# Storing one chunk last, with its MoE rows added by one-hot matmuls, in a channel-attention and mixture-of-depths kernel

## Chip, cores and metric

The kernel runs on one core of a Trainium2 chip. The metric is the device time of one execution in microseconds (us), the median of several runs. The core has TensorE (PE; its weight loads are listed apart as PEld), VectorE (DVE), ScalarE (ACT), GpSimd (POOL) and SyncE (SP), which work side by side and wait for each other by semaphores, and 16 DMA engines, which all transfers share.

## What is computed

Four batches of q, k and v, each 6208 rows by 256 channels, go through attention among the channels. The result goes through a mixture-of-depths layer: in each batch, the 128 rows with the highest score get an MLP added.

```python
# B, N, C = 4, 6208, 256;  F = 1024;  capacity = 128
qn = q / (norm(q, axis=1) + 1e-6);  kn = k / (norm(k, axis=1) + 1e-6)
a = softmax(kn.transpose(0, 2, 1) @ qn / tau)     # 256 x 256 for each batch
x = v @ a
scores = x @ w_gate
out = x.copy()
for b in range(B):
    top = indices of the 128 highest scores[b]
    xe = x[b, top]
    ye = maximum(xe @ w1, 0) @ w2
    out[b, top] = xe + sigmoid(scores[b, top])[:, None] * ye
```

## The kernel before

A batch has six chunks of 1024 rows (8 rows in each of 128 partitions) and a rest of 64 rows. Pass 1 reads q and k and accumulates k'q and the norms. A softmax of 256 x 256 follows. Pass 2 reads v, transposes it, multiplies it by the attention matrix `a_sb`, and stages the rows for the store. Beside that a selection (a search for the threshold in 7 steps on VectorE, with a small matmul in each) finds the 128 rows of the batch. They are gathered from v, go through the MLP, and are scattered over the rows that are already stored. So a scatter must come after the stores of its own batch.

All loads are issued by GpSimd and cast from float32 to bfloat16 on the way. All stores are issued by SyncE. GpSimd issues strictly in the order of the program.

```python
QK_BUFS = 4;  V_BUFS = 6;  ST_BUFS = 7;  EARLY = 4;  HOLD = 3
...
T = [("T", L, g, a) for g, a in zip(gs, [1, 1, 1, 0, 1, 1, 0, 1, 0, 1, 0, 1, 0])]  # transposes, last batch
S = [("S", L, g) for g in gs]                                                       # its scores
plan += [("tail",)] + T[:2] + [("warm", L, 6)] + T[2:3] + [("warm", L, 6)] + T[3:4]
plan += [("adv",), ("a", L)]
for i in range(4, 7):
    plan += [T[i], ("warm", L, 8)]
plan += [T[7], ("warm", L, 4), T[8], T[9]] + S[:4] + [("warm", L, 4)] + T[10:] + [("side",)] + S[4:]
...
def emit_weights():                       # issued by GpSimd behind the first loads of q and k
    nc.gpsimd.dma_start(out=w1_sb, in_=moe_w1.rearrange("(dc p) f -> p dc f", p=P))
    nc.gpsimd.dma_start(out=w2_sb, in_=moe_w2.rearrange("(fc p) d -> p fc d", p=P))
...
def keep_warm(n):                         # matmuls whose result nobody reads
    bank = ps_o.tile([P, 2, C], F32, name="o_ps")
    for _ in range(n):
        nc.tensor.matmul(bank[:, 0, 0:P], lhsT=ident_b, rhs=ones_b, start=True, stop=True)
...
def between():                            # after each pair of output rows: a step of the selection or MLP
    if now[0] > B:
        pairs[0] += 1
        if pairs[0] % 5 in (0, 3) and not advance(side):
            advance_all(side2)
...
# pass 2: outputs of two rows of each partition at a time
for pj in range(m):
    for cc in range(2):
        nc.tensor.matmul(o_ps[:parts, pj, :], lhsT=vt_sb[:, cc, j, :parts], rhs=a_sb[:, cc, :], ...)
if now[0] > B and not side and pairs[0] % 2 == 1:
    nc.vector.tensor_copy(st[...], o_ps[:parts, :m, :])
else:
    nc.scalar.copy(st[...], o_ps[:parts, :m, :])
between()
...
# the end of the MLP of batch b
upd = moe.tile([P, D], F32, name="upd", bufs=2)
nc.vector.scalar_tensor_tensor(out=upd, in0=y_ps[:, 0, :], scalar=gate, in1=xe, op0=ALU.mult, op1=ALU.add)
yield
yield
while held[b] or (b >= E - 1 and deferred):
    yield
nc.gpsimd.indirect_dma_start(out=out_flat[0:(b + 1) * N, :],
                             out_offset=bass.IndirectOffsetOnAxis(ap=idx[:, 0:1], axis=0), in_=upd, ...)
...
# the tail, after the last loads of v
b = B - 1
side.append(select_stages(b))
advance(side)
flush_deferred()                          # the stores held back: three of batch 1, two of batch 2
...
now[0] = B + 1
pairs[0] = 1
for op in rest:                           # outputs of batch 2 (E) from the third chunk on
    do_out(E, op[2], False)
for g in gs:                              # outputs of batch 3
    do_out(b, g, False)
while side:
    advance(side)
...
keep_warm(32)
while side2:                              # MLP and scatter of batch 3
    advance(side2)
```

Of the kernel before, what the change touches and what calls it, by code (L numbers as in the profile page):

```python
# [9 lines left out]
F32 = mybir.dt.float32  # L10
BF16 = mybir.dt.bfloat16
# [6 lines left out]
P = 128  # L18
# [8 lines left out]
def kernel(  # L27
# [72 lines left out]

    gs = [g for ci in range(NFULL + 1) for g in groups(ci)]
    E = B - 2

    def mixed(b, ci, extra):

# [7 lines left out]
    def pass2(b):  # L113
        ops = [("T", b, gs[0], 1), ("T", b, gs[1], 1), ("a", b)]
        for i, g in enumerate(gs):
            ops.append(("O", b, g, True))
# [24 lines left out]

    T = [("T", L, g, a) for g, a in zip(gs, [1, 1, 1, 0, 1, 1, 0, 1, 0, 1, 0, 1, 0])]
    S = [("S", L, g) for g in gs]
    plan += [("tail",)] + T[:2] + [("warm", L, 6)] + T[2:3] + [("warm", L, 6)] + T[3:4]
    plan += [("adv",), ("a", L)]
    for i in range(4, 7):
        plan += [T[i], ("warm", L, 8)]
    plan += [T[7], ("warm", L, 4), T[8], T[9]] + S[:4] + [("warm", L, 4)] + T[10:] + [("side",)] + S[4:]
    units = []
    for op in plan:  # L150
        if op[0] in ("p1", "T"):
# [51 lines left out]

    pump(4)


    ident_f = const.tile([P, P], F32)
    make_identity(nc, ident_f)
# [46 lines left out]
    ones_col = const.tile([P, NCOL], BF16)  # L255
    nc.vector.memset(ones_col, 1.0)

    w1_sb = const.tile([P, C // P, F], BF16)
    w2_sb = const.tile([P, NFC, D], BF16)

    def emit_weights():
        nc.gpsimd.dma_start(out=w1_sb, in_=moe_w1.rearrange("(dc p) f -> p dc f", p=P))
        nc.gpsimd.dma_start(out=w2_sb, in_=moe_w2.rearrange("(fc p) d -> p fc d", p=P))

    pump()
    emit_weights()


    acc = {}
# [28 lines left out]
    def softmax_stages(b):  # L298
        s_ps, g_ps = acc[b]
        s_sb = smx.tile([P, 2, C], F32, name="s_sb")  # L300
        nc.scalar.copy(s_sb, s_ps)  # L301
        junk = smx.tile([P, P], F32, name="junk")
        nsq = smx.tile([P, 4], F32, name="nsq")
        for i in range(4):
            nc.vector.tensor_tensor_reduce(out=junk, in0=g_ps[:, i, :], in1=ident_f, scale=1.0,  # L305
                                           scalar=0.0, op0=ALU.mult, op1=ALU.add,
                                           accum_out=nsq[:, i:i + 1])


# [29 lines left out]
        e = smx.tile([P, 2, C], F32, name="e")  # L339
        rsum = smx.tile([P, 2], F32, name="rsum")  # L340
        aw = smx.tile([P, 2], F32, name="aw")
        for cc in range(2):
            ss = smx.tile([P, C], F32, name=f"ss{cc}")
            nc.vector.tensor_tensor(out=ss, in0=s_sb[:, cc, :], in1=rq_ps[:, 0:C], op=ALU.mult)
            nc.scalar.activation(e[:, cc, :], ss, AF.Exp, scale=rn[:, 2 + cc:3 + cc],
                                 accum_out=rsum[:, cc:cc + 1])
# [19 lines left out]
    stage_of = {}  # L366
    deferred = []
    gate_done = []
    held = {b: NFULL + 1 for b in range(B)}
    side = []  # L370
    side2 = []
    waiting = []
# [19 lines left out]
    def p2_transpose(b, g, on_act=False):  # L392
        ci, s0, n = g
        parts = P if ci < NFULL else REM
        vt = loaded[("v", b, ci)][0]
        vt_ps = vt_psum()
        for j in range(n):
            for cc in range(2):
                nc.tensor.transpose(vt_ps[:, cc, j, :parts], in_=vt[:parts, s0 + j, cc * P:(cc + 1) * P],  # L399
                                    identity=ident_b[:parts, :parts])  # L400
        vt_sb = vt_pool.tile([P, 2, 4, P], BF16, name="vt_sb")
# [51 lines left out]
    def p2_out(b, g, vt_sb, scores):  # L453
# [9 lines left out]
        for pair in range((n + 1) // 2):  # L463
# [13 lines left out]
                nc.scalar.copy(st[:parts, s0 + pair * 2:s0 + pair * 2 + m, :], o_ps[:parts, :m, :])  # L477
            between()

    def emit_store(b, ci):  # L480
        st = stage_of.pop((b, ci))
        if ci < NFULL:
            return nc.sync.dma_start(out=view(out, b, ci), in_=st)
        return nc.sync.dma_start(out=view(out, b, ci), in_=st[:REM, 0, :])


    gathered = {}

    def select_stages(b):

# [97 lines left out]
    def mlp_stages(b):  # L588
# [44 lines left out]
        for fc in range(NFC):  # L633
            nc.tensor.matmul(y_ps[:, 0, :], lhsT=h_sb[:, fc, :], rhs=w2_sb[:, fc, :], start=fc == 0,
                             stop=fc == NFC - 1)
        upd = moe.tile([P, D], F32, name="upd", bufs=2)
        nc.vector.scalar_tensor_tensor(out=upd, in0=y_ps[:, 0, :], scalar=gate, in1=xe, op0=ALU.mult,
                                       op1=ALU.add)
        yield
        yield  # L640
        while held[b] or (b >= E - 1 and deferred):
            yield
        nc.gpsimd.indirect_dma_start(out=out_flat[0:(b + 1) * N, :],
                                     out_offset=bass.IndirectOffsetOnAxis(ap=idx[:, 0:1], axis=0),
                                     in_=upd, in_offset=None)


    smx_side = []
# [85 lines left out]
    for op in plan:  # L734
# [16 lines left out]
        elif kind == "a":  # L751
            while b not in a_tiles:
                advance(smx_side)
        elif kind == "side":
            while side:
                advance(side)
# [66 lines left out]
```

## Time and profile before

| what | value |
|---|---|
| time, median of 3 runs (lowest to highest) | 269.53 us (269.02 to 269.69) |
| span of the profiled run | 266.5 us |
| TensorE busy | 203.4 us (76% of the span) |
| VectorE busy | 119.9 us (45%) |
| ScalarE busy | 76.7 us (29%) |
| GpSimd busy | 57.2 us (21%) |
| moved by the DMA engines | 65.92 MB, mean 247 GB/s |
| read from HBM, written to HBM | 79.04 MB, 25.95 MB |

The page divides the span into 40 slices of 6.66 us; each digit is the busy share of a slice in tenths. GB/s counts the bytes that the transfers deliver, so a load that casts float32 to bfloat16 counts half of what it reads. In the chain of waits, each line is a start, a duration and what was waited for; it runs back from the last instruction to what released it. A "stretch" is a part of the span between two times, with the busy time of each engine, the granted share of TensorE's clock, the DMA share and GB/s. "POOLq" and "SPq" are the sequencers of those engines, which wait and issue and are not counted as busy.

### The profile page before, as it was taken

What the parts mean: (1) busy time and instruction counts of PE and PEld (TensorE: products, weight loads), DVE (VectorE), ACT (ScalarE), POOL (GpSimd) and SP (SyncE); (2) the same over time, 40 slices, a digit from 0 to 9 for tenths busy, and PEclk for the clock granted to TensorE, in tenths of its full rate; (3) what the DMA queues carried; (4) which work ended last, traced back from release to release, by engine and by line L of the source; (5) the groups of instructions that cost most, each with busy time, mean ns of one, the idle gap of its engine ahead of it and who ended that gap; (6) DMA issues with size and microseconds to landing.
All of it is one profiled execution on the core that took longest, in us unless ns stands there. A gap on an engine that the chain in (4) does not pass through costs nothing.

```text
span 266.5 us, 6120 instructions
## 1 busy us (share of the span) xinstructions
PE 203.4 (76%) x2604; PEld 179.1 (67%) x2604; DVE 119.9 (45%) x466; ACT 76.7 (29%) x140; POOL 57.2 (21%) x106
## 2 busy tenths in 40 slices
PE   0587278899965866799997896899998798899710
PEld 0476267789954656689986785889987586678500
DVE  0200001714415356614438845774866745867500
ACT  1000000157730000137651001533004545885300
POOL 7322213121110023222201343220431011010110
PEclk9999959999989799799997999999999985899995
DMA  6999999999999999999999999999999999999920
GB/s 112 214 211 209 213 212 211 215 213 264 314 317 313 312 218 214 215 213 224 318 314 228 212 218 218 212 215 213 213 209 214 202 361 404 421 408 406 419 76 0
DMA packets 17642, 65.92 MB, mean 247 GB/s; under 512 B 2000, under 2 KB 4688, under 8 KB 14544
## 3 DMA queue, kind: packets, MB, share of 16 engines
q0 software_dynamic: 13696, 39.98, 76.0%
q1 hardware_dynamic: 3920, 25.56, 23.6%
q8 instruction: 20, 0.33, 0.4%
q14 instruction: 6, 0.05, 0.0%
HBM read 79.04 MB, written 25.95 MB: 394 GB/s over the span
## 4 chain that ended last, share of the span: by engine, by line
DMA 54%; PE 23%; issue 9%; DVE 7%; POOL 2%; ACT 1%; POOLq 1%; SPq 0%
DMA k_ch<-in_k_dram 29%; DMA q_ch<-in_q_dram 17%; DMA v_ch<-in_v_dram 6%; PE s_ps L286 5%; PE o_ps L469 5%; DMA out_dram<-stage_rem 3%; PE g_ps L290 2%; PE g_ps L288 2%; PE vt_ps L399 2%; PE s_ps L469 2%; PE sc_ps L424 1%; DVE cnt L532 1%; PE g_ps L469 1%; DVE cmp L528 1%; DVE junk L305 1%
## 5 line engine op out<-in xcount | busy, mean ns | idle before, releaser
L286 PE MATMUL s_ps<-q_ch,k_ch 128*128 128x256 bf16 x384 | 96.0, 290 | 30.1 <-DMA k_ch<-in_k_dram 28.9
L288 PE MATMUL g_ps<-q_ch 128*128 128x128 bf16 x384 | 88.3, 230 | 1.6 <-DVE nsq L305 1.6
L290 PE MATMUL g_ps<-k_ch 128*128 128x128 bf16 x384 | 88.2, 230 | 0.0
L286 PEld LDWEIGHTS <-k_ch 128*128 128x128 bf16 x384 | 39.9, 104 | 34.7 <-DMA k_ch<-in_k_dram 31.8
L469 PE MATMUL o_ps<-a_sb,vt_sb 128*128 128x256 bf16 (+1 forms) x310 | 47.6, 279 | 1.5 <-ACT vt_sb L403 1.3
L477 ACT COPY stage<-o_ps 128x512 f32<-128x512 f32 x76 | 42.8, 588 | 19.7 <-PE o_ps L469 17.2
L290 PEld LDWEIGHTS <-k_ch 128*128 128x128 bf16 x384 | 39.9, 104 | 8.8 <-issue 2.1
L288 PEld LDWEIGHTS <-q_ch 128*128 128x128 bf16 x384 | 39.9, 104 | 1.7 <-issue 1.4
L469 PEld LDWEIGHTS <-vt_sb 128*128 128x128 bf16 x392 | 32.2, 101 | 9.0 <-issue 3.5
L405 DVE COPY vt_sb<-vt_ps 128x1024 bf16<-128x1024 bf16 (+1 forms) x35 | 22.2, 637 | 31.9 <-PE vt_ps L399 31.8
L301 ACT COPY s_sb<-s_ps 128x512 f32<-128x512 f32 x4 | 2.3, 586 | 105.9 <-PE s_ps L286 105.9
L424 PEld LDWEIGHTS <-vt_sb 128*128 128x128 bf16 x392 | 25.4, 97 | 2.7 <-DVE u L495 0.2
L399 PEld LDWEIGHTS <-v_ch 128*128 128x128 bf16 x384 | 22.3, 97 | 5.9 <-DMA v_ch<-in_v_dram 4.7
L399 PE MATMUL vt_ps<-ident_b,v_ch 128*128 128x128 bf16 x336 | 24.7, 219 | 1.6 <-DMA v_ch<-in_v_dram 0.9
L424 PE MATMUL sc_ps<-aw_sb,vt_sb 128*128 128x2 bf16 x392 | 25.8, 164 | 0.0
L305 DVE CUSTOM_DVE_ANT_0 junk<-g_ps,ident_f 128x128 f32<-128x128 f32 x16 | 4.7, 291 | 41.8 <-PE g_ps L290 41.4
L174 POOL DMA_DIRECT2D q_ch<-in_q_dram x23 | 12.8, 555 | 49.1 <-PE g_ps L290 18.5
L174 POOL DMA_DIRECT2D k_ch<-in_k_dram x23 | 12.6, 546 | 27.9 <-DMA k_ch<-in_k_dram 8.8
L174 POOL DMA_DIRECT2D v_ch<-in_v_dram x24 | 12.8, 539 | 24.2 <-DMA k_ch<-in_k_dram 11.5
L532 DVE TENSOR_REDUCE cnt<-cmp 128x7 bf16<-128x343 bf16 x28 | 14.4, 513 | 1.0
L528 DVE SCALAR_TENSOR_TENSOR cmp<-u,delta,shares 128x343 bf16<-128x343 f32 x24 | 13.9, 579 | 0.9
L403 ACT COPY vt_sb<-vt_ps 128x1024 bf16<-128x1024 bf16 x11 | 10.6, 1012 | 12.3 <-PE vt_ps L399 12.2
(138 smaller groups left out, 199.8 us busy)
## 6 DMA issues: line engine op xcount, KB each, us to landing
out_dram<-stage SPq DMA_DIRECT2D x24, 1024.0 KB, 9.1
v_ch<-in_v_dram POOLq DMA_DIRECT2D x24, 512.0 KB, 14.9
q_ch<-in_q_dram POOLq DMA_DIRECT2D x23, 512.0 KB, 17.2
k_ch<-in_k_dram POOLq DMA_DIRECT2D x23, 512.0 KB, 18.5
w_sb<-in_moe_w_dram POOLq DMA_DIRECT2D x2, 512.0 KB, 19.9
q_ch<-in_q_dram POOLq DMA_DIRECT2D x2, 256.0 KB, 9.7
k_ch<-in_k_dram POOLq DMA_DIRECT2D x2, 256.0 KB, 10.4
out_dram<-stage_rem SPq DMA_DIRECT2D x4, 64.0 KB, 6.7
```

The source lines that it names most:

```text
L174: ins = nc.gpsimd.dma_start(out=t, in_=view(src, b, ci))
L286: nc.tensor.matmul(s_ps[:, cc, :], lhsT=ks[:, sl], rhs=qs, start=first and cc == 0, stop=last and cc == 1)
L288: nc.tensor.matmul(g_ps[:, cc, :], lhsT=qs[:, sl], rhs=qs[:, sl], start=first and cc == 0, stop=False)
L290: nc.tensor.matmul(g_ps[:, 2 + cc, :], lhsT=ks[:, sl], rhs=ks[:, sl], start=False, stop=last and cc == 1)
L399: nc.tensor.transpose(vt_ps[:, cc, j, :parts], in_=vt[:parts, s0 + j, cc * P:(cc + 1) * P], identity=ident_b[:parts, :parts])
L403: nc.scalar.copy(vt_sb[:, :, :n, :parts], vt_ps[:, :, :n, :parts])
L405: nc.vector.tensor_copy(vt_sb[:, :, :n, :parts], vt_ps[:, :, :n, :parts])
L424: nc.tensor.matmul(sc_ps[:parts, col, :], lhsT=vt_sb[:, cc, j, :parts], rhs=aw_sb[:, cc, :], start=cc == 0 and col in (0, NCOL - 1), stop= ...
L469: nc.tensor.matmul(o_ps[:parts, pj, :], lhsT=vt_sb[:, cc, j, :parts], rhs=a_sb[:, cc, :], start=pj == 0 and cc == 0, stop=pj == m - 1 and ...
L477: nc.scalar.copy(st[:parts, s0 + pair * 2:s0 + pair * 2 + m, :], o_ps[:parts, :m, :])
L528: nc.vector.scalar_tensor_tensor(out=cmp, in0=wide, scalar=delta, in1=thr, op0=ALU.subtract, op1=ALU.is_ge)
L532: nc.vector.tensor_reduce(out=cnt, in_=cmp, axis=AX.X, op=ALU.add)
```

## The change

Four things are changed together.

1. One chunk of batch 1, the last full one, is not computed in pass 2 of its batch. Its transposed v is kept in a buffer of its own (`vt_late`). Its outputs are computed in the tail, and its store is issued last of all, behind the stores of batch 3. The scatter of batch 1 runs before that store, so the store must bring the MoE rows with it: for each of the 8 rows of a partition, a one-hot matrix of 128 x 128 says which selected row belongs there, and three matmuls of it with the MLP's result, split into three bfloat16 parts, are added to the outputs in PSUM. The purpose is that the transfers have something to do while the last scatter waits for the stores of batch 3.
2. The MoE weights are loaded in float32 by SyncE ahead of everything into two staging buffers, and ScalarE casts them.
3. A store and a scatter of different batches are declared independent.
4. The dummy matmuls of the tail are fewer (the one-hot pairs stand in their place), the selection of the last batch takes its steps sooner, and the softmax works in place, which frees space.

```diff
-    plan += [("tail",)] + T[:2] + [("warm", L, 6)] + T[2:3] + [("warm", L, 6)] + T[3:4]
-    plan += [("adv",), ("a", L)]
-    for i in range(4, 7):
-        plan += [T[i], ("warm", L, 8)]
-    plan += [T[7], ("warm", L, 4), T[8], T[9]] + S[:4] + [("warm", L, 4)] + T[10:] + [("side",)] + S[4:]
+    plan += [("tail",)] + T[:2] + [("late", H, 0)] + T[2:4] + [("adv",), ("a", L)]
+    plan += T[4:8] + [("late", H, 1)] + T[8:10] + S[:4] + [("warm", L, 4)] + T[10:] + [("side",)] + S[4:]
...
+    def emit_weights():
+        for dst, src, inner in ((w1_sb, moe_w1, F), (w2_sb, moe_w2, D)):
+            raw = st_pool.tile([P, RPP, C], F32, name="stage").rearrange("p a c -> p (a c)")
+            raw = raw.rearrange("p (k n) -> p k n", n=inner)
+            nc.sync.dma_start(out=raw, in_=src.rearrange("(k p) n -> p k n", p=P))
+            nc.scalar.copy(dst, raw)
+    emit_weights()
...
-            if pairs[0] % 5 in (0, 3) and not advance(side):
+            due = pairs[0] in (2, 4, 6) or pairs[0] > 6 and pairs[0] % 5 in (0, 3)
+            if due and not advance(side):
...
+    def late_pair(k):
+        ...
+        for pj in range(2):
+            for cc in range(2):
+                nc.tensor.matmul(o_ps[:, pj, :], lhsT=vts[(H, g)][:, cc, k % 2 * 2 + pj, :], rhs=a_sb[:, cc, :],
+                                 start=pj == 0 and cc == 0, stop=False)
+            for i in range(3):
+                nc.tensor.matmul(o_ps[:, pj, :], lhsT=onehot[:, row + pj, :], rhs=parts[:, i, :],
+                                 start=False, stop=pj == 1 and i == 2)
+        nc.scalar.copy(st[:, row:row + 2, :], o_ps)
+    def late_rows(b, idx, gy):
+        base = float(b * N + (NFULL - 1) * CHUNK)
+        at = moe.tile([P, 1], F32, name="late_at")
+        nc.gpsimd.tensor_copy(at, idx)
+        nc.gpsimd.tensor_scalar(out=at, in0=at, scalar1=-base, scalar2=1.0 / RPP, op0=ALU.add, op1=ALU.mult)
+        at_row = moe.tile([P, RPP], F32, name="late_at_row")
+        nc.gpsimd.tensor_scalar(out=at_row, in0=iota_row[:, 0:RPP], scalar1=-1.0 / RPP, scalar2=at, ...)
+        onehot = moe.tile([P, RPP, P], BF16, name="late_onehot")
+        for s in range(RPP):
+            nc.gpsimd.tensor_scalar(out=onehot[:, s, :], in0=iota_row, scalar1=at_row[:, s:s + 1], ..., op0=ALU.is_equal)
+        parts = moe.tile([P, 3, D], BF16, name="late_parts")
+        for i in range(3):
+            nc.gpsimd.tensor_copy(parts[:, i, :], gy)
+            if i < 2:
+                nc.gpsimd.tensor_tensor(out=gy, in0=gy, in1=parts[:, i, :], op=ALU.subtract)
...
+        for o, sca in scatters:
+            if o != b:
+                tc.declare_no_dep(ins.ins, sca.ins, reason="rows of different batches")
...
-        nc.vector.scalar_tensor_tensor(out=upd, in0=y_ps[:, 0, :], scalar=gate, in1=xe, op0=ALU.mult, op1=ALU.add)
+        if b == H:                            # H = batch 1
+            gy = moe.tile([P, D], F32, name="gy")
+            nc.vector.tensor_scalar(out=gy, in0=y_ps[:, 0, :], scalar1=gate, scalar2=None, op0=ALU.mult)
+            nc.gpsimd.tensor_tensor(out=upd, in0=gy, in1=xe, op=ALU.add)
+            late_rows(b, idx, gy)
+        else:
+            nc.vector.scalar_tensor_tensor(...)
...
     side.append(select_stages(b))
     advance(side)
+    advance(side)
     flush_deferred()
...
-    pairs[0] = 1
     for op in rest:
         do_out(E, op[2], False)
-    for g in gs:
+    for i, g in enumerate(gs):
         do_out(b, g, False)
+        if i in (8, 9):
+            late_pair(i - 6)
+    emit_store(H, NFULL - 1)
...
-    keep_warm(32)
+    keep_warm(8)
```

More of the change, by code (lines that the diff above doesn't have):

```diff
@@ L102 @@
     E = B - 2
+    H = B - 3
+    late = [(NFULL - 1, 0, 4), (NFULL - 1, 4, 4)]
     def mixed(b, ci, extra):
@@ L115, in pass2 @@
         for i, g in enumerate(gs):
-            ops.append(("O", b, g, True))
+            ops.append(("S", b, g) if b == H and g in late else ("O", b, g, True))
             if i + 2 < len(gs):
@@ L204 @@
     pump(4)
+    w1_sb = const.tile([P, C // P, F], BF16)
+    w2_sb = const.tile([P, NFC, D], BF16)
+    def emit_weights():
+        for dst, src, inner in ((w1_sb, moe_w1, F), (w2_sb, moe_w2, D)):
+            assert C * F == P * RPP * C
+            raw = st_pool.tile([P, RPP, C], F32, name="stage").rearrange("p a c -> p (a c)")
[3 more added lines that the diff above has]
+    emit_weights()
     ident_f = const.tile([P, P], F32)
@@ L256 @@
     nc.vector.memset(ones_col, 1.0)
[L258 to L263, printed above, removed]
     pump()
-    emit_weights()
     acc = {}
@@ L338, in softmax_stages @@
                          start=True, stop=True)
-        e = smx.tile([P, 2, C], F32, name="e")
+        e = s_sb
         rsum = smx.tile([P, 2], F32, name="rsum")
@@ L342, in softmax_stages @@
         for cc in range(2):
[L343 to L345 removed]
+            nc.vector.tensor_tensor(out=e[:, cc, :], in0=e[:, cc, :], in1=rq_ps[:, 0:C], op=ALU.mult)
+            nc.scalar.activation(e[:, cc, :], e[:, cc, :], AF.Exp, scale=rn[:, 2 + cc:3 + cc],
                                  accum_out=rsum[:, cc:cc + 1])
@@ L368 @@
     gate_done = []
-    held = {b: NFULL + 1 for b in range(B)}
+    held = {b: NFULL + 1 - (b == H) for b in range(B)}
     side = []
@@ L400, in p2_transpose @@
                                     identity=ident_b[:parts, :parts])
-        vt_sb = vt_pool.tile([P, 2, 4, P], BF16, name="vt_sb")
+        if b == H and g in late:
+            vt_sb = moe.tile([P, 2, 4, P], BF16, name="vt_late", bufs=2)
+        else:
+            vt_sb = vt_pool.tile([P, 2, 4, P], BF16, name="vt_sb")
         if on_act:
@@ L478, in p2_out @@
             between()
+    def late_pair(k):
+        g = late[k // 2]
+        onehot, parts = late_moe
+        if k == 0:
+            stage_of[(H, NFULL - 1)] = st_pool.tile([P, RPP, C], F32, name="stage")
+        st = stage_of[(H, NFULL - 1)]
+        a_sb = a_tiles[H][0]
+        o_ps = out_psum()
+        row = g[1] + k % 2 * 2
+        for pj in range(2):
[6 more added lines that the diff above has]
+        nc.scalar.copy(st[:, row:row + 2, :], o_ps)
@@ new lines @@
+    late_moe = []
+    def late_rows(b, idx, gy):
[4 more added lines that the diff above has]
+        at_row = moe.tile([P, RPP], F32, name="late_at_row")
+        nc.gpsimd.tensor_scalar(out=at_row, in0=iota_row[:, 0:RPP], scalar1=-1.0 / RPP, scalar2=at,
+                                op0=ALU.mult, op1=ALU.add)
+        onehot = moe.tile([P, RPP, P], BF16, name="late_onehot")
+        for s in range(RPP):
+            nc.gpsimd.tensor_scalar(out=onehot[:, s, :], in0=iota_row, scalar1=at_row[:, s:s + 1],
+                                    scalar2=None, op0=ALU.is_equal)
+        parts = moe.tile([P, 3, D], BF16, name="late_parts")
[3 more added lines that the diff above has]
+                nc.gpsimd.tensor_tensor(out=gy, in0=gy, in1=parts[:, i, :], op=ALU.subtract)
+        late_moe.extend([onehot, parts])
@@ L480, in emit_store @@
     def emit_store(b, ci):
         st = stage_of.pop((b, ci))
-        if ci < NFULL:
-            return nc.sync.dma_start(out=view(out, b, ci), in_=st)
-        return nc.sync.dma_start(out=view(out, b, ci), in_=st[:REM, 0, :])
+        ins = nc.sync.dma_start(out=view(out, b, ci), in_=st if ci < NFULL else st[:REM, 0, :])
+        stores.append((b, ins))
+        for o, sca in scatters:
+            if o != b:
+                tc.declare_no_dep(ins.ins, sca.ins, reason="rows of different batches")
@@ L487 @@
+        return ins
     gathered = {}
+    stores = []
+    scatters = []
     def select_stages(b):
@@ L636, in mlp_stages @@
         upd = moe.tile([P, D], F32, name="upd", bufs=2)
-        nc.vector.scalar_tensor_tensor(out=upd, in0=y_ps[:, 0, :], scalar=gate, in1=xe, op0=ALU.mult,
-                                       op1=ALU.add)
+        if b == H:
[3 more added lines that the diff above has]
+            late_rows(b, idx, gy)
+        else:
+            nc.vector.scalar_tensor_tensor(out=upd, in0=y_ps[:, 0, :], scalar=gate, in1=xe, op0=ALU.mult,
+                                           op1=ALU.add)
         yield
@@ L642, in mlp_stages @@
             yield
-        nc.gpsimd.indirect_dma_start(out=out_flat[0:(b + 1) * N, :],
-                                     out_offset=bass.IndirectOffsetOnAxis(ap=idx[:, 0:1], axis=0),
-                                     in_=upd, in_offset=None)
+        ins = nc.gpsimd.indirect_dma_start(out=out_flat[0:(b + 1) * N, :],
+                                           out_offset=bass.IndirectOffsetOnAxis(ap=idx[:, 0:1], axis=0),
+                                           in_=upd, in_offset=None)
+        scatters.append((b, ins))
+        for o, sto in stores:
+            if o != b:
+                tc.declare_no_dep(ins.ins, sto.ins, reason="rows of different batches")
     smx_side = []
@@ L753 @@
                 advance(smx_side)
+        elif kind == "late":
+            late_pair(op[2])
         elif kind == "side":
```

## The prediction

> **What bounds the kernel now.** I read the 40 slices first, then the DMA part of the page, then the chain of waits, then the stretches and single tiles. The DMA row of the slices and the row of GB/s under it:
>
> ```profile
> DMA  6999999999999999999999999999999999999920
> GB/s 112 214 211 209 213 212 211 215 213 264 314 317 313 312 218 214 215 213 224 318 314 228 212 218 218 212 215 213 213 209 214 202 361 404 421 408 406 419 76 0
> ```
>
> The 16 DMA engines are full from the second slice to slice 38. At 210-215 GB/s they load (casting to bf16, so the bytes read are twice that); at 400-420 they only store. So nothing on a compute engine counts by itself: a microsecond is won or lost only where the DMA engines stand idle. There are three such places. The stretches (columns: engines' busy time, then TensorE's granted clock, DMA share, GB/s) show two of them:
>
> ```profile
> 2.00:4.00 2.00, 0.00 (x0) 0.00 (x0) 0.00 (x0) 0.08 (x1) 2.00 (x5) 1.00 0.84 98
> 212.00:214.00 2.00, 1.64 (x30) 1.47 (x28) 0.69 (x1) 1.01 (x1) 0.00 (x0) 1.00 0.69 133
> 215.00:254.00 39.00, 34.37 (x371) 27.32 (x367) 24.40 (x88) 22.83 (x43) 3.98 (x4) 0.87 1.02 410
> ```
>
> At the start 98 GB/s instead of 213; at the turn from loads to stores 133. Then 39 us of stores without a gap. The third place is the end, in the chain of waits:
>
> ```profile
> 248.62 0.02 SPq L484
> 248.64 0.03 issue
> 248.67 7.21 DMA out_dram<-stage_rem
> 255.88 0.02 issue
> ...
> 256.12 0.54 issue
> 256.66 1.19 POOLq L818
> ```
>
> The last store of batch 3 lands at 255.88; only then may its 128 MoE rows be scattered over it. In the list of the engines' instructions:
>
> ```profile
> 253.56 0.33 PEld L634 LDWEIGHTS <-h_sb 128*128 128x128 bf16 x4 [0.15 <-ACT h_sb L629]
> 254.21 0.48 DVE L637 SCALAR_TENSOR_TENSOR upd<-o_ps,gate,xe 128x256 f32<-128x256 f32 x1 [1.54 <-PE o_ps L634]
> 256.88 0.97 POOL L643 DMA_INDIRECT out_dram<-upd,idx  x1 [9.39 <-issue]
> ```
>
> The scatter starts at 256.88, 1.0 us after the store landed; the view of its tile gives 2.4 us to landing, so 259.3. From there to the end of the span (266.5) is 7.2 us of closing work that the change does not touch. Note `upd`: done at 254.69, only 1.2 us ahead of the landing it then waits for. That is all the slack the MoE chain of batch 3 has.
>
> **What the Trainium skill says.** (1) "DMA: Bandwidth & Descriptors", section "Issuing engines are not separate DMA queues": transfers of all issuing engines run on the same 16 DMA engines and interleave. So moving the weights to the hardware queue removes no transfer, it only starts one earlier. The trace agrees that the engines are one pool: loads fall behind while stores run beside them (slices at 313-318 GB/s in total). (2) "GPSIMD Engine Reference", section "Performance versus the Vector engine": a two-input elementwise operation costs GpSimd about 2.6 cycles an element at 1.2 GHz. No such operation is in the kernel before, so its trace cannot say. (3) The same page, "Specifications": GpSimd's SBUF interfaces are shared with VectorE; no stretch of this trace has both at work long enough to show it. (4) "TensorE: Matmul & The Clock Gate", Part 1: the clock is halved by idle windows of some 3.4 us and given back after a busy one. The trace agrees: the granted clock is 0.50 in every microsecond from 218 to 228 and 1.00 after it.
>
> **The change, part by part.**
>
> *Weights.* Two casting transfers of 0.52 MB (2.45 us each at 213 GB/s) become two of 1.05 MB at about 410 GB/s (2.55 us each): equal. But SyncE issues its first transfer at 0.81, GpSimd at 1.33 after which its packets take until about 4.3 to flow. From 1.9 to 4.3 (2.4 us) the engines now move some 0.13 MB of gate weights and 0.11 MB of q, worth 0.3 + 0.5 us at full rate. Filled with weights that stretch wins at most 1.6 us; some ramp stays. I take **-1.2 us**. The first q and k chunks land later (they share the engines), but TensorE has 30 us of idle time waiting for k in this kernel, so it catches up.
>
> *Work of GpSimd.* Ahead of the two halves of the last full q,k chunk in GpSimd's order now stand 14 instructions: one add 256 wide, 3 small ones, 8 one-hots of 128x128, 3 copies and 2 subtractions 256 wide. One-input 128x128 operations take 0.24-0.31 us there (memset, iota and selects of the setup): 8 x 0.3 = 2.4; copies of 256 about 0.45 x 3 = 1.35; three two-input ones at 256 x 2.6 / 1.2 GHz + 0.15 = 0.7 each = 2.1 (an estimate from the page named under (2)); the small ones 0.45; waits between them some 0.6: **about 7 us**. They can start when the MoE product of batch 1 is ready, in the trace before at 188.1, so they end at 195. Now these loads are issued from 187.59 on:
>
> ```profile
> 187.59 0.53 POOL L183 DMA_DIRECT2D q_ch<-in_q_dram  x1 [10.31 <-PE g_ps L290]
> ```
>
> The load issued before them (k at 176.74) takes 18.5 us to landing, so the engines have work until 195.2. An issue at 195 needs 1.3 us until its bytes move: the engines run dry from 195 to 196. I take **+0.8 us** (0 if GpSimd is quick, 2 if the selection on VectorE, which shares its interfaces, slows it).
>
> *The tail.* Of the five stores held back for it, four remain, as the sixth chunk of batch 1 moves to the very end. So the engines get 2.55 us less of ready work at 214, while TensorE makes new chunks at half clock. Before, the first computed chunk was issued at 223.76 and landed 8.4 us later, the second at 228.33 and landed 6.3 later; alone a chunk needs 1.1 + 2.55 + 0.4 = 4.05 (issue to first byte as in SyncE's first transfer, the bytes, last byte to landing as in the last scatter). So the slack in the queue was 4.3 and 2.3 us, and 2.55 of it goes. Moreover the selection's first matmul now stands ahead of the outputs: TensorE waits for VectorE about 1 us there and 0.9 us at the next count, which makes the first chunk 1.9 us later and the second 0.8. Slacks: 4.3-2.55-1.9 = -0.2, then 2.3-2.55-0.8 = -1.05; the worst of them counts, and with the next two chunks like the second I put the gap at about 1.5 us in all. The engines thus end at 254.3 + 1.5 = 255.8, now with the late chunk as the last.
>
> *The end.* Batch 3's own stores end a chunk earlier, at 255.9 - 2.55 + 1.5 = 254.8. But its MoE chain moves too. After the last outputs (247.7 before) stand 32 dummy matmuls and then 5.2 us of MoE. The 24 dropped dummies give back 24 x 0.056 = 1.35 (32 weight loads in 1.79 us). The one-hot pairs among the outputs cost 20 matmuls x 0.11 = 2.2 (four outputs take 0.44 in the chain); the selection ends four pairs earlier in order, which only swaps waits for outputs. Outputs end at about 250, `upd` at 250 + 0.45 + 5.2 = 255.7. With about 0.6 for the issue and 2.4 to landing: 258.7 against 259.3. So the MoE chain replaces the store as the last wait, and the part meant to win 2.55 us wins **-0.6 us**; the late store (255.8 + 0.4) hides under it.
>
> The one-hot pairs of the first half and the dummies they replace are equal (20 x 0.11 against 40 x 0.056 us) and lie in waits for v. The in-place softmax saves space, no time. The freed waits of scatters free nothing the chain shows.
>
> Sum: -1.2 + 0.8 - 0.6 = -1.0.
>
> **The rivals.** *(A) The end as intended:* the clock comes back one window (3.4 us, 1.7 us of work) sooner, the gaps close and the MoE chain is done first: then 1.7 more, and -2.7 in all. For it: the selection runs sooner, the pairs of 256 columns are solid work; against: the sparse score matmuls that dropped the clock are still there. *(B) The loads run dry:* GpSimd takes 10 us or more, the last loads come 3 us late, everything after shifts; +1.5 in all. For it: VectorE does the selection just then, over shared interfaces; against: one-input operations are quick in this trace. *(C) Starved tail:* half clock for one window longer, stores trickle: +1. *(D) All hidden:* start, GpSimd and tail cancel: 0.
>
> **Range and chances.** I lean a little to A over C (0.4 against 0.15 of the 1.7 us each): -1.0 - 0.4 = -1.4, so 269.5 - 1.4 = 268.1. A plus a full start and no dry spell would be 269.5 - 1.6 - 2.3 = 265.6; B and C together 269.5 + 1.5 + 1 = 272, which I hold unlikely. Range 265.3 to 270.6. Faster by over 2% needs below 264.1, more than the start and the end can give together (1.6 + 3.4 = 5.0): 0.08. Slower by over 2% needs 5.4 us of starvation: 0.03.
>
> **What would show it.** Right at the start: a stretch 2 to 4 near 200 GB/s or above. The GpSimd step: time between its add and the issue of the half chunk near 7 us, and a DMA share under 0.9 in one or two microseconds around 195. The tail: a share clearly under 1 between 224 and 236. The end: a chain that comes through the MoE of batch 3 and not through a store. Wrong would be: the last store as the end of the chain, a dry spell of over 2 us, or a full clock through the tail.

## The result, and the profile after

The changed kernel takes 276.44 us (median of four, 275.5 to 281.8) against 269.36 before: ratio 1.024, 95% interval 1.021 to 1.028. A second measurement, which shares its runs of the kernel before with two of the experiments, gives 276.47 against 268.58, ratio 1.030 (1.027 to 1.032). So the change makes the kernel 6.5 to 8 us slower; predicted was 268.1, 1.4 faster. The profile shown here is of the second measurement (span 274.6); that of the first was of a slower execution (span 280.0), in which GpSimd's work began later (191.8) and the hole described below is longer.

The DMA rows of the 40 slices of the changed kernel, read as in the prediction:

```profile
DMA  6999999999999999999999999999299998899950
GB/s 220 230 227 228 213 213 212 213 215 318 316 313 314 252 213 213 214 212 277 310 279 213 211 223 213 214 212 211 43 165 211 212 358 313 354 386 402 381 230 0
```

Before, the row was at 9 from the second slice to slice 38. Now there is a hole in slice 29 (43 GB/s), a slow slice behind it (165), and the storing slices have fallen from 404-421 to 313-402. The first slice is better, 220 instead of 112. Stretches (busy time of each engine, TensorE's granted clock, DMA share, GB/s):

```profile
2.00:4.00 2.00, 0.00 (x0) 0.00 (x0) 0.00 (x0) 0.07 (x1) 2.00 (x5) 1.00 0.75 262
...
192.00:194.00 2.00, 2.00 (x28) 1.74 (x26) 1.63 (x7) 0.00 (x0) 2.00 (x5) 1.00 0.53 107
194.00:196.00 2.00, 1.09 (x16) 1.03 (x16) 0.75 (x5) 0.00 (x0) 1.77 (x4) 1.00 0.06 10
196.00:198.00 2.00, 2.00 (x29) 1.82 (x28) 1.83 (x6) 0.00 (x0) 1.94 (x4) 1.00 0.00 0
198.00:200.00 2.00, 0.80 (x12) 0.59 (x9) 0.95 (x3) 0.00 (x0) 2.00 (x5) 1.00 0.75 108
200.00:202.00 2.00, 0.00 (x0) 0.00 (x0) 0.00 (x0) 0.00 (x0) 1.31 (x3) 1.00 1.02 176
202.00:204.00 2.00, 0.87 (x7) 0.75 (x8) 0.00 (x0) 0.00 (x0) 1.06 (x2) 0.67 1.09 158
204.00:206.00 2.00, 2.00 (x17) 1.69 (x16) 0.72 (x5) 0.00 (x0) 0.53 (x1) 0.50 1.15 178
206.00:208.00 2.00, 1.74 (x24) 1.49 (x23) 0.52 (x4) 0.00 (x0) 1.00 (x2) 0.97 1.06 202
```

The fifth busy column is GpSimd: nearly full (1.77 to 2.00 of 2 us) through the whole hole, while the DMA engines have nothing. What it does there (start, duration, engine, line, operation):

```profile
187.21 0.73 POOL L694 TENSOR_TENSOR upd<-gy,xe 128x256 f32<-128x256 f32 x1 [10.26 <-DVE ge L596]
...
189.17 4.82 POOL L520 TENSOR_SCALAR late_onehot<-iota_row,late_at_row 128x128 bf16<-128x128 f32 x8
...
196.89 0.67 POOL L182 DMA_DIRECT2D q_ch<-in_q_dram  x1
```

The first of the four loads that bring the last full chunk of q and k in halves ("the half chunk" from here on), issued at 187.59 before, is issued at 196.89, 9.7 us after GpSimd began. Counting each stretch from 192 to 208 by its GB/s against 213, the engines lose 1.0 + 1.9 + 2.0 + 1.0 = 5.9 us up to 200 and 1.3 us more in a slow restart (176, 158, 178 and 202 GB/s): 7.2 us. Less the 1.0 us won at the start, that is the delay of the last load: it lands at 222.47 instead of 216.13, 6.3 us later.

The end of the chain of waits, and then the last instructions of the MoE of batch 3:

```profile
258.00 0.61 PE o_ps L418 x8
258.73 5.08 DMA out_dram<-stage_rem
263.96 0.54 issue
264.50 1.21 POOLq L887
```

```profile
263.12 0.48 DVE L697 SCALAR_TENSOR_TENSOR upd<-o_ps,gate,xe 128x256 f32<-128x256 f32 x1 [1.53 <-PE o_ps L688]
264.72 0.98 POOL L703 DMA_INDIRECT out_dram<-upd,idx  x1 [10.94 <-DMA out_dram<-stage_rem]
```

The scatter is issued at 264.72 (256.88 before, 7.8 us later). Of these, 6.3 us were there when the loads ended; the tail added 1.5. The last store of batch 3 lands at 263.8 and `upd` is done at 263.60: the store is still the last wait, as the releaser in the line says, but the two now end within 0.2 us of each other, where before the MoE chain had 1.2 us to spare.

### The profile page after: what moved, and what is told of

It is laid out like the page before. It is cut to its first block, busy times and chain, and to the rows that moved or that the text cites. A ratio compares the mean times of both kernels' runs of the same rounds, so it can differ in the third digit from the quotient of the medians.

```text
span 280.0 us, 6063 instructions
## 1 busy us (share of the span) xinstructions
PE 206.2 (74%) x2564; PEld 180.2 (64%) x2564; DVE 122.9 (44%) x469; ACT 79.4 (28%) x139; POOL 65.8 (24%) x121
## 4 chain that ended last, share of the span: by engine, by line
DMA 44%; PE 28%; DVE 12%; issue 7%; POOL 4%; ACT 1%; POOLq 1%; DVEq 0%
DMA k_ch<-in_k_dram 28%; DMA v_ch<-in_v_dram 11%; PE o_ps L476 7%; PE s_ps L290 5%; PE vt_ps L402 3%; DMA q_ch<-in_q_dram 3%; DVE cnt L586 2%; PE g_ps L294 2%; PE g_ps L292 2%; DMA out_dram<-stage_rem 2%; DVE cmp L582 2%; POOL late_onehot L520 2%; PE sc_ps L430 2%; PE g_ps L476 1%; PE s_ps L476 1%
## 5 line engine op out<-in xcount | busy, mean ns | idle before, releaser
L290 PE MATMUL s_ps<-q_ch,k_ch 128*128 128x256 bf16 x384 | 98.3, 295 | 40.4 <-DMA k_ch<-in_k_dram 39.2
L292 PE MATMUL g_ps<-q_ch 128*128 128x128 bf16 x384 | 89.5, 233 | 1.4 <-DVE nsq L309 1.4
L294 PE MATMUL g_ps<-k_ch 128*128 128x128 bf16 x384 | 89.5, 233 | 0.0
L290 PEld LDWEIGHTS <-k_ch 128*128 128x128 bf16 x384 | 40.5, 106 | 45.8 <-DMA k_ch<-in_k_dram 42.7
L294 PEld LDWEIGHTS <-k_ch 128*128 128x128 bf16 x384 | 40.6, 106 | 9.3 <-issue 1.9
L476 PE MATMUL o_ps<-a_sb,vt_sb 128*128 128x256 bf16 x294 | 45.2, 279 | 1.4 <-ACT vt_sb L409 1.3
L484 ACT COPY stage<-o_ps 128x512 f32<-128x512 f32 x64 | 36.0, 588 | 16.1 <-PE o_ps L476 15.3
L476 PEld LDWEIGHTS <-vt_sb 128*128 128x128 bf16 (+1 forms) x376 | 30.9, 101 | 8.6 <-issue 3.5
L411 DVE COPY vt_sb<-vt_ps 128x1024 bf16<-128x1024 bf16 (+1 forms) x33 | 20.8, 634 | 29.7 <-PE vt_ps L402 29.7
L430 PEld LDWEIGHTS <-vt_sb 128*128 128x128 bf16 (+1 forms) x376 | 24.0, 98 | 2.5 <-DVE u L549 0.2
L430 PE MATMUL sc_ps<-aw_sb,vt_sb 128*128 128x2 bf16 (+1 forms) x376 | 24.3, 164 | 0.0
L582 DVE SCALAR_TENSOR_TENSOR cmp<-u,delta,shares 128x343 bf16<-128x343 f32 x24 | 14.7, 611 | 0.9
L409 ACT COPY vt_sb<-vt_ps 128x1024 bf16<-128x1024 bf16 x11 | 10.6, 1012 | 12.3 <-PE vt_ps L402 12.3
```

Source lines behind the costliest of these rows:

```text
L290: nc.tensor.matmul(s_ps[:, cc, :], lhsT=ks[:, sl], rhs=qs, start=first and cc == 0, stop=last and cc == 1)
L292: nc.tensor.matmul(g_ps[:, cc, :], lhsT=qs[:, sl], rhs=qs[:, sl], start=first and cc == 0, stop=False)
L294: nc.tensor.matmul(g_ps[:, 2 + cc, :], lhsT=ks[:, sl], rhs=ks[:, sl], start=False, stop=last and cc == 1)
L430: nc.tensor.matmul(sc_ps[:parts, col, :], lhsT=vt_sb[:, cc, j, :parts], rhs=aw_sb[:, cc, :], start=cc == 0 and col in (0, NCOL - 1), stop= ...
L582: nc.vector.scalar_tensor_tensor(out=cmp, in0=wide, scalar=delta, in1=thr, op0=ALU.subtract, op1=ALU.is_ge)
```

## The experiments

Times are given as the difference of the median to that of the kernel before in the same set of runs.

**The work of GpSimd moved to VectorE (e_dve).** The first theory: the instructions on GpSimd ahead of the last loads are the cause. (The prediction and the expectations call them 14; the list they give, and the kernel, have 17: one add, 3 small ones, 8 one-hots, 3 copies, 2 subtractions.) The rival: the whole tail, fewer stores in hand and a slower first chunk.

```diff
-        nc.gpsimd.tensor_copy(at, idx)            # and the other 16, line by line
+        nc.vector.tensor_copy(at, idx)
```

> The changed kernel with the 14 instructions that make the one-hot rows (add, 3 small ones, 8 one-hots, 3 copies, 2 subtractions) on VectorE in place of GpSimd; nothing else differs. Theory (the dry spell: GpSimd stands in front of the last loads of q and k, and the DMA engines run dry behind it): the half chunk is issued near 188 as before, no stretch around 195 to 203 below a DMA share of 0.9, time 269 to 271.5. Rival (the tail: one store less in hand, a store more at the end, 20 matmuls more): the dry spell was only shifted waiting, time stays at 275 or more.

Measured 270.88, +1.9 (ratio 1.008, 1.005 to 1.011). Against the changed kernel's +7.9 the placement of these instructions is worth 6.0 us. VectorE needs half the time for a one-hot. The eight in the view of their tile, first of this run, then of the changed kernel (shortest, median and longest duration in ns, then the first and the last start):

```profile
L520 DVE TENSOR_SCALAR late_onehot<-iota_row,late_at_row x8: 281/283/350, 188.2 to 189.5; 128x128 bf16<-128x128 f32 x8
```

```profile
L520 POOL TENSOR_SCALAR late_onehot<-iota_row,late_at_row x8: 595/616/640, 189.2 to 193.4; 128x128 bf16<-128x128 f32 x8
```

The half chunk is issued at 186.55 and there is no hole. The remaining loss is in the tail. The issue, then stretches of the same run:

```profile
186.55 0.53 POOL L182 DMA_DIRECT2D q_ch<-in_q_dram  x1 [9.62 <-PE g_ps L294]
...
194.00:196.00 2.00, 2.00 (x19) 1.74 (x18) 0.60 (x2) 0.00 (x0) 0.53 (x1) 0.59 1.12 210
...
215.00:259.00 44.00, 36.26 (x393) 28.80 (x391) 28.17 (x96) 24.27 (x44) 3.96 (x4) 0.88 0.91 361
224.00:228.00 4.00, 3.30 (x18) 2.37 (x18) 3.29 (x12) 2.04 (x4) 0.00 (x0) 0.50 0.29 84
```

Share 0.91 over 44 us, where the kernel before had 1.02 over 39: (1.02 - 0.91) x 44 = 4.8 us of engine time not used.

**The work left on GpSimd, but behind the last load (e_behind).** If being ahead of the loads is what costs, the same work on the same engine is cheap once it stands behind them.

```diff
-            late_rows(b, idx, gy)                 # in the MoE step of batch 1
+            put_off.append((upd, gy, xe, b, idx))
 ...
+            late_rows(b1, idx1, gy1)              # after the last load is issued
-  ... + [("late", H, 0)] + ... + [("late", H, 1)] + T[8:10] + S[:4] + [("warm", L, 4)]
+  ... + [("warm", L, 20)] + ... + [("warm", L, 20)] + T[8:10] + S[:4] + [("late", H, 0), ("late", H, 1)]
```

> The changed kernel with the same 14 instructions still on GpSimd, but behind the issue of the last load of v; the one-hot pairs of the first half move behind the first scores, dummies fill their old places. Theory (dry spell): 269 to 272, no dry stretch before the tail. Rival (the work of GpSimd itself, or its sharing with VectorE, or the tail costs the time): 275 or more.

Measured 271.11, +2.1 (ratio 1.009, 1.006 to 1.012): the same as on VectorE within the noise. GpSimd's one-hots take the same 0.60 us there, but no load stands behind them. So neither GpSimd's work in itself nor its sharing with VectorE costs the 6 us.

**No late chunk (e_nolate), and the weights alone (e_weights).** These take the sum apart from both ends: the change without its main part, and the kernel before with only the weights moved.

```diff
-    late = [(NFULL - 1, 0, 4), (NFULL - 1, 4, 4)]
+    late = []                                     # e_nolate; the first two late pairs become 20 dummies each
```

> The changed kernel without the late chunk: all chunks stored as before, no one-hots; the weights on the hardware queue, the independent scatters, the earlier selection and the in-place softmax stay. Theory (dry spell): these four cost and win little, 268.5 to 270. Rival (one of these four costs the time): 274 or more.

> The kernel before with the weights alone moved to the hardware queue. Prediction's step: 1.2 us faster, 268.2. Rival read from the profile after (the transfers at the start mix badly; the eighth load lands at 29.92 against 30.02 with the weights): 0 to 0.5 us faster, 269 to 269.4. Second rival (the weights delay the first chunks and with them everything): over 271.

e_nolate: 269.57, +0.6 (ratio 1.0016, 1.0001 to 1.0031). e_weights: 267.96, -1.0 (0.9962, 0.9947 to 0.9978). Its stretch at the start:

```profile
2.00:4.00 2.00, 0.00 (x0) 0.00 (x0) 0.00 (x0) 0.10 (x1) 2.00 (x5) 1.00 0.73 260
```

260 GB/s instead of 98, the picture of the full change. So the weights keep what they promised, and something besides the late chunk costs 1.6 us. (In e_nolate the last store of batch 1 and the fused update of its MoE are as before again, and the two one-hot pairs of the tail are gone.)

**The hole put into the kernel before (b_block, b_half).** The same kind of instructions with idle results, ahead of the same loads: 15 (without two of the small ones), and 6.

```diff
+        if b == B - 3:
+            nc.gpsimd.tensor_tensor(out=blk, in0=upd, in1=xe, op=ALU.add)
+            nc.gpsimd.tensor_copy(blk_row, iota_row[:, 0:RPP])
+            for s in range(8):                    # b_half: range(2)
+                nc.gpsimd.tensor_scalar(out=blk_b[:, 0:P], in0=iota_row, scalar1=blk_row[:, s:s + 1],
+                                        scalar2=None, op0=ALU.is_equal)
+            for i in range(3):                    # b_half: range(1)
+                ...                               # copy to bf16, subtract
```

> The kernel before with idle work of the same kind put into GpSimd's order where the changed kernel has its own: one add, a small copy, 8 one-hots of 128 x 128, 3 copies and 2 subtractions of 256, into scratch, read by nobody. Theory (dry spell): some 9 us from 188.1 on, so the last loads are issued at 197 and move at 198.5, while the engines have work until 195: about 3.5 us dry, time 272 to 274. Rival (what costs is the late chunk in the tail, not GpSimd): 269 to 270.

> The same, with a third of the work: one add, one small copy, 2 one-hots, one copy, one subtraction, about 3.3 us. Theory (dry spell, so a threshold): it ends near 191.5, the loads move before 195, nothing is lost: 268.7 to 269.8. Rival (GpSimd's work costs in proportion, by its sharing with VectorE or by delay handed on): a third of what the full block costs, 1 to 1.5 us.

b_block: 278.35, +9.5 (ratio 1.034, 1.029 to 1.038), far above the 272 to 274 expected: its hole is also longer than the changed kernel's.

```profile
190.14 0.73 POOL L643 TENSOR_TENSOR blk<-upd,xe 128x256 f32<-128x256 f32 x1 [13.35 <-DVE ge L542]
...
191.40 6.16 POOL L646 TENSOR_SCALAR blk_b<-iota_row,blk_row 128x128 bf16<-128x128 f32 x8
...
200.70 0.63 POOL L183 DMA_DIRECT2D q_ch<-in_q_dram  x1
```

It began at 190.1, 2 us later than expected, took 10.6 us (two of its one-hots took 0.93 us; why is not known) and released the loads at 200.70, 3.8 us after the changed kernel. Counted as above, its stretches from 192 to 210 lose 10.5 us. b_half: 270.55, +1.7 (ratio 1.008, 1.005 to 1.011), above the theory's 269.8, where a slack of some 7 us should have swallowed its 3.7 us. It issued the half chunk at 193.03, still 2 us ahead of the 195.2 at which I had the engines run dry; its stretches:

```profile
192.00:194.00 2.00, 2.00 (x31) 1.90 (x29) 1.90 (x7) 0.00 (x0) 1.92 (x4) 1.00 0.62 123
194.00:196.00 2.00, 2.00 (x31) 1.90 (x29) 1.64 (x6) 0.00 (x0) 2.00 (x5) 1.00 0.79 112
```

From 192 on the engines carry 123 GB/s: the transfers in flight thin out some 3 us before the last of them lands, and the slack ends there. After it the rate stays at 168, 169 and 172 GB/s until 202, though the engines never ran dry (94 GB/s in the slowest half microsecond). From 192 to 204 the profiled run, one of 271.48 us, loses 3.1 us in this way. The run refutes my way of counting the slack. It is nearer to the rival's 1 to 1.5 us, but that was a third of a cost put at 3 to 4.5; of b_block's 9.5 it is 0.18, for a third of the work, and e_behind speaks against a cost of the work itself.

**The old pace of the selection (e_pace; e_nolate_pace).** The 1.6 us that belong neither to the weights nor to the late chunk: the suspect is the selection of batch 3, which the change puts ahead of the outputs.

```diff
-            due = pairs[0] in (2, 4, 6) or pairs[0] > 6 and pairs[0] % 5 in (0, 3)
-            if due and not advance(side):
+            if pairs[0] % 5 in (0, 3) and not advance(side):
 ...
-    advance(side)                                 # the second of two
+    pairs[0] = 1
```

> The changed kernel with the one-hots on VectorE (270.9) and the selection of the last batch at its old pace: no second step ahead of the outputs, steps as before. Theory (the earlier selection holds up the first outputs of the tail, and the engines run dry for 3.5 us before the first computed chunk): the first computed chunk is issued near 224 in place of 227, time 268.5 to 270. Rival (the missing fifth store alone makes the dry stretch): 270.5 to 271.5.

> The change without the late chunk and with the old pace of the selection. If the earlier selection is what cost 1.6 us between the weights alone and the version without a late chunk, this is 267.6 to 268.3, equal to the weights alone (267.96), and the first computed chunk is stored near 224 instead of 227.2. If the fewer dummy matmuls or the freed waits cost it, it stays at 269.3 or more.

e_pace (on top of e_dve): 268.51, -0.4 (ratio 0.998, 0.996 to 1.000), 2.3 us less than e_dve. e_nolate_pace (on top of e_nolate): 268.08, -0.5 (0.998, 0.997 to 0.999), 1.1 us less than e_nolate and within 0.5 of the weights alone. The runs of e_pace vary more than others, most of them anywhere between 266.7 and 270.2. TensorE of e_nolate, and then of e_nolate_pace, at the end of the scores:

```profile
217.79 1.97 PE L430 MATMUL sc_ps<-aw_sb,vt_sb 128*128 128x2 bf16 x66
221.28 0.77 PE L557 MATMUL m_ps<-ident_f,mx 128*128 128x128 f32 x2 [1.53 <-DVE mx L554]
221.84 1.06 PE L476 MATMUL s_ps<-a_sb,vt_sb 128*128 128x256 bf16 x4
```

```profile
217.20 1.89 PE L430 MATMUL sc_ps<-aw_sb,vt_sb 128*128 128x2 bf16 x66
219.02 0.61 PE L475 MATMUL s_ps<-a_sb,vt_sb 128*128 128x256 bf16 x4
219.47 0.60 PE L475 MATMUL o_ps<-a_sb,vt_sb 128*128 128x256 bf16 x4
```

With the early selection TensorE waits 1.53 us for VectorE's maximum before its first output; with the old pace two groups of outputs fill that wait. Together with a score phase 0.7 us later, and with the counts in between, the first computed chunk is stored at 227.24 instead of 223.81. Five stores in hand don't last so long: the share of 215 to 255 is 0.99, against 1.02 with the old pace.

**One more store in hand (e_hold).** If the late chunk hurts by taking a held store away, hold another back (on top of e_pace).

```diff
-    HOLD = 3
+    HOLD = 4
```

> The last kernel, and four chunks of batch 1 held back in place of three counted with the late one, so that five stores are in hand at the turn as before. Theory (both the pace and the missing store made the tail dry, and hiding a store under the last scatter is worth up to 2.5 us): no stretch of the tail under a share of 0.7, time 266 to 268, so faster than before by 1 to 3 us. Rival (the MoE chain of batch 3 sets the end whatever the stores do): 268 to 269.5.

Measured 269.08, +0.2 (ratio 0.999, 0.997 to 1.001): a miss, no gain, and inside the rival's range. The turn now comes at 210.15, as a store left the loading phase; but TensorE is still in its first pass over batch 3 until 208.7, and the first computed chunk is not ready until 226.09. Stretches of this run:

```profile
224.00:228.00 4.00, 3.02 (x16) 1.98 (x15) 3.50 (x13) 2.03 (x4) 0.00 (x0) 0.50 0.59 202
229.00:231.00 2.00, 1.58 (x15) 1.21 (x14) 1.59 (x7) 1.66 (x3) 0.00 (x0) 0.91 0.16 66
```

The hole in the tail only moved: TensorE's work between the turn and the first chunk takes 15.9 us (its clock 1.00 until 222, 0.50 from 223 on), longer than five stores last. At the end the store and the chain are level: the last store of batch 3 lands at 257.93, `upd` is done at 257.96.

**The dummies back (e_warm).** Does the MoE chain of batch 3 set the end? On top of e_pace:

```diff
-    keep_warm(8)
+    keep_warm(32)
```

> One-hots on VectorE, old pace of the selection, and all 32 dummy matmuls back behind the last outputs. The 24 take 24 x 0.056 = 1.3 us at full clock. If the MoE chain of batch 3 sets the end, the time is 268.51 + 0.7 to 1.3 = 269.2 to 269.8; if the late store or the last store of batch 3 sets it, 268.51 stays within 0.4; if the dummies keep the clock up for the MoE matmuls, it falls to 267.5 to 268.

Measured 269.22, +0.6 (ratio 1.001, 1.000 to 1.003), 1.0 us more than e_pace when each is taken against its own before. That fits the MoE chain as the last wait once the dummies are back, and the trace says so by name. The tail of this run, which has the late chunk and the old pace, follows as a stretch:

```profile
255.88 0.48 DVE L696 SCALAR_TENSOR_TENSOR upd<-o_ps,gate,xe 128x256 f32<-128x256 f32 x1 [1.54 <-PE o_ps L687]
256.64 0.97 POOL L702 DMA_INDIRECT out_dram<-upd,idx  x1 [8.57 <-DVE upd L696]
...
215.00:256.00 41.00, 35.69 (x417) 28.95 (x416) 26.04 (x93) 25.12 (x47) 3.96 (x4) 0.96 0.97 386
```

The last store of batch 3 had landed at 255.00, 1.4 us before `upd`; 24 dummies of 0.056 us are 1.3 of that. The first computed chunk was stored at 224.0, as e_pace's theory said for the old pace.

**The changed kernel once more (a_again)** gave the profile shown above.

> The changed kernel as it is, once more, for a profile of an ordinary execution. If the work of GpSimd ahead of the last loads is the cause (5.6 us by the experiment that moves the same instructions to VectorE), the span comes out at 272 to 275, the half chunk is issued within 1 us of the end of GpSimd's 14 instructions, these take 9.5 to 10.5 us, and the DMA share is under 0.2 for 5 us or more before that issue. If the gap seen in the first profile belonged to that slower execution alone, it is under 3 us here.

Measured 276.47, +7.9; span 274.6; 9.7 us of GpSimd, and the half chunk issued at its end. The hole is shorter than I wrote down: under 0.2 for some 4 us, from 194 to 198.

**The one-hot by itself (b_setup).** Is 0.60 us the operation, or VectorE beside it on shared interfaces (rival B of the prediction)? Five operations in the setup of the kernel before, where VectorE is idle.

```diff
+    nc.gpsimd.tensor_scalar(out=trial[:, 0, :], in0=iota_row, scalar1=iota_col[:, 0:1], ..., op0=ALU.is_equal)
+    ...                                           # once more; against the constant 3.0; a copy; fp32 out
```

> The kernel before with five operations of 128x128 put on GpSimd in the setup, between 10.8 and 15.2 us, where GpSimd has nothing to do and VectorE is idle: two one-hots against a column of scalars, one comparison with a constant, one plain copy to bf16, one one-hot kept in fp32. If the one-hots cost 0.60 us in the changed kernel because VectorE (83% busy there) shares GpSimd's memory interfaces, they take 0.30 to 0.40 us here. If it is the operation itself, they take 0.58 to 0.62 here too; if the column of scalars is what costs, the comparison with a constant and the copy take 0.30 or less; if the conversion to bf16 costs, the fp32 one is the short one. The time of the kernel stays that of before, 268.6 plus or minus 0.7.

```profile
10.91 0.63 POOL L269 TENSOR_SCALAR trial<-iota_row,iota_col 128x128 bf16<-128x128 f32 x1
11.51 0.61 POOL L271 TENSOR_SCALAR trial<-iota_row,iota_col 128x128 bf16<-128x128 f32 x1
12.10 0.52 POOL L273 TENSOR_SCALAR trial<-iota_row 128x128 bf16<-128x128 f32 x1
12.57 0.28 POOL L275 CAST trial<-iota_row 128x128 bf16<-128x128 f32 x1
12.85 0.59 POOL L276 TENSOR_SCALAR trial_f<-iota_row,iota_col 128x128 f32<-128x128 f32 x1
```

The operation itself. A copy of that size takes 0.28 us, a comparison with a constant 0.52, one with a column of scalars 0.59 to 0.63, whatever the output's type. VectorE, idle here, has no part in the 0.60. The time was +0.6 (ratio 1.002, 1.000 to 1.004). The sharing of rival B does show in the changed kernel, but the other way round, and with GpSimd's two-input operations. VectorE's comparison of two tiles takes 0.58 us beside the one-hots, 1.08 beside the add (b_block and b_half: 1.07) and 0.88 beside the second subtraction (at 195.81):

```profile
187.24 1.08 DVE L582 SCALAR_TENSOR_TENSOR cmp<-u,delta,shares 128x343 bf16<-128x343 f32 x1
...
189.33 0.58 DVE L582 SCALAR_TENSOR_TENSOR cmp<-u,delta,shares 128x343 bf16<-128x343 f32 x1
```

That is 0.8 us of VectorE's time, small beside the 6 us.

## Why the prediction was wrong

The differences, one step at a time, from the kernel before to the changed one: weights -1.0 (e_weights); fewer dummies, in-place softmax and freed scatters +0.5 (e_nolate_pace); the early selection +1.1 (e_nolate); the late chunk with its one-hots on VectorE +1.3 (e_dve); the same on GpSimd ahead of the loads +6.0. Together +7.9; each step is uncertain by some 0.4 to 1 us. The third and the fourth belong together: with the late chunk in place the early selection costs 2.3 (e_dve against e_pace).

*Weights, -1.2.* Right: -1.0. 260 GB/s in the stretch 2 to 4, as said.

*Work of GpSimd, +0.8.* This is the step that failed: +6.0. Its mechanism, a blocked queue and engines that run dry, was right; three terms were mis-sized, all in the same direction, and the dry spell was about 4 us where over 2 us was the sign of being wrong. (1) "One-input 128x128 operations take 0.24-0.31 us": a comparison against a column of scalars takes 0.60 (b_setup), so the eight cost 4.8 us and not 2.4; the three small ones took 0.97 and not 0.45, and the whole 9.7 us and not "about 7 us". I took the duration from memsets, selects and iotas, because they have the same shape and one input; the operation decides. The two-input ones were estimated right from the Trainium skill, "GPSIMD Engine Reference", section "Performance versus the Vector engine": 0.7 us each, 0.67 to 0.73 measured in the changed kernel. (2) "The engines have work until 195.2": the last landing is not the last moment of full use. At 192 to 194 the rate was already 107 GB/s here, and b_half, which released the loads at 193.03, paid 1.7 us. (3) "An issue needs 1.3 us until its bytes move": they did move, but at 158 to 202 GB/s until 208, which costs 1.3 us more. This low rate is not explained by the dry spell: b_half, whose engines never ran dry, has it too. The start of GpSimd's work, 188.1 in my text, was 187.21. So 5.9 us of hole and 1.3 us of restart stand where I had 0.8. Rival B named the size of the work ("10 us or more"), but for a reason that b_setup refutes, and gave it +1.5 in all.

*The tail, a gap of 1.5 us.* Right in kind, too small. With the loads undisturbed (e_dve) the unused engine time is 4.8 us; with the old pace 2.1 us remain (e_warm, share 0.97 over 41 us), and without the late chunk none (e_nolate_pace, share 1.02 over 39 us). I had put the early selection at 1.9 us for the first chunk and 0.8 for the next; for the first it was 3.4 (227.24 against 223.81). The half clock came as foreseen (0.50 from 224 to 228 in e_dve), but "idle windows" are not what the trace of the kernel before shows ahead of it: from 214 to 218 TensorE is busy 3.6 of 4 us, 91%, and from 218 the clock is 0.50.

*The end, -0.6.* The turn-over was half right: the two waits come level, and neither clearly replaces the other. The last store ends later by 0.2 us in the changed kernel, which was named as a sign of being wrong, and by 0.6 in e_dve; the MoE chain ends later by 0.3 in e_behind, and clearly (1.4) only in e_warm, which has 24 dummies more in it. And no gain is left: as the gap in the tail was larger, the chain as a whole came 1.5 us later after the end of the loads, not earlier. The late store itself is hidden, as predicted: in e_dve it landed at 261.09 and the scatter at 262.05. e_pace against e_nolate_pace shows what the late chunk is worth with the selection at its old pace and no work on GpSimd: +0.1, each against its own before and each uncertain by 0.3 to 0.6, so nothing that can be told from zero. It takes a store (2.55 us by the prediction's estimate) off the path of batch 3, and puts 2.2 us of matmuls on TensorE in front of the MoE chain and one store less into the turn.

*The chances.* 5.4 us of starvation for a slowdown of over 2% had the chance 0.03; the loading phase alone brought 7.2. Rivals B and C came together, and B at four times the size I gave it.

What stays open: why the loads come at 158 to 178 GB/s after a late issue, and the +0.5 between e_weights and e_nolate_pace, which is not divided further. Nothing was found that is faster than e_weights (267.96, 0.4% ahead of before). No run tried a smaller one-hot, or one built as soon as the rows are known, before the MoE product.

## What to carry to other kernels

An engine that issues transfers is part of the transfer path: before putting arithmetic on it, look for the next load in its order and count backward from the moment when the rate begins to fall, not from the last landing. Take an instruction's duration from the same operation with the same operands, or measure it alone where the kernel has idle time; shape and number of inputs aren't enough. Taking a piece off the last wait pays at most the slack of the chain that becomes the next last wait (1.2 us here), less what the change adds to that chain (here 2.2 us of matmuls, against 1.3 us of dropped dummies), so measure that slack first.

## What was not expected of the hardware

GpSimd's comparison of 128x128 took 0.52 to 0.63 us, about twice its plain copy (0.28) and, for the one-hots, twice the time on VectorE (0.283). With only the last few transfers in flight the DMA engines fell from 213 to 107-123 GB/s about 3 us before the end of the work that I had counted on, and after a dry spell of 4 us it was 206, 8 us after the first bytes, before a stretch reached 202 GB/s again; b_half shows 168 to 172 GB/s for 6 us without a dry spell. The Trainium skill, "DMA: Bandwidth & Descriptors", section "Issuing engines are not separate DMA queues", says that transfers of all engines interleave on the same 16; the runs agree (weights on either queue, only the start moves), but the order of issue within one engine decided some 6 us here.
